# Interleaved state-space layers: residual and gate sums by accumulating DMA, another operand order in a short convolution, norm statistics by tile

## The chip, the cores and the metric

One core of a Trainium2 chip runs the whole program. Its engines work side by side, each through its own queue in order: TensorE (PE; weight loads are listed apart as PEld), VectorE (DVE), ScalarE (ACT), GpSimd (POOL) and SyncE (SP, which here only issues DMAs). The metric is the device time of one execution in microseconds. A profile is one execution recorded by the hardware; its span runs from the first to the last instruction.

## The reference

The input x has 2048 tokens of 640 channels. Four residual layers follow each other, A, B, A, B, with the same weights in both rounds:

```python
x = x + A(layernorm(x));  x = x + B(layernorm(x));  x = x + A(layernorm(x));  x = x + B(layernorm(x))

# A: diagonal complex recurrence over tokens, 640 states
Lam_bar = exp(exp(log_dt) * Lam);  B_bar = ((Lam_bar - 1) / Lam)[:, None] * Bmat
h_t = Lam_bar * h_(t-1) + B_bar @ u_t;  A(u)_t = 2 * real(Cmat @ h_t) + u_t * Dskip

# B: gate by a long convolution that does not depend on x
k_shift = causal convolution of k with shift_k (4 taps);  kv = k_shift * v
B(u) = u * (causal convolution of kv with ssm_k (2048 taps) + kv * ssm_D)
```

Since the gate of B does not depend on x, it is computed once ("the y part") and used by both B layers.

## The kernel before, in words

**Order.** Nothing is scheduled while the program is built. Every piece of work is a named task with an engine, and the string `ORDER` lists the tasks; `Sched.run` emits them in that order, so each engine's queue is the order's subsequence. A suffix `/a` or `/d` puts an evacuation or a normalise on ACT or DVE. `PLACE` gives every buffer its place in one SBUF arena, and every PSUM buffer its banks. Both were written out ahead by a planner; the numbers beside the tasks (estimates, `LAT`, `DMA`, and `SWD` in the change) were its costs and are not used when the program is built.

**The y part** works in five slices of 128 channels (`y_pass`, names `yq0` to `yq4`). First the short convolution and the product with v are made (`kv_tasks`, names `kv_`): k and v are loaded transposed, channels on partitions; per slice and half of the tokens eight products of 512 columns (L1025) with a diagonal matrix of one tap as stationary operand are summed in PSUM, and DVE multiplies by v (L1031). The result goes to a scratch tensor `kvd` in DRAM (`kv_st`, L1035) and comes back (`yqN_vl`, L1124) with 128 consecutive tokens of one channel to a row, a layout in which a Fourier transform can be done by matrix products: stage A with a small table `FA` (L1063, products that use 64 rows of the array), stage B with cosines and sines (L1087 to L1092). The same is done for ssm_k, the spectra are multiplied on DVE (L1138 to L1143), transformed back (L1162, L1163, an on-chip transpose, L1190), and stored to `ysd`. The table `FA` is made by POOL, DVE and ACT (`yt_f0` to `yt_f4`).

**The A layers** (`ALayer.chunk`, names `A1cN_` and `A2cN_`) work in four chunks of 512 tokens, and a chunk has four tiles q of 128 tokens on partitions and 640 channels. Statistics of a tile give the norm (`_ln`), `_id` applies it, a DMA transposes the chunk (`_tu`), `_bp` multiplies by the input weights (L635, L638), `_ev` evacuates, DVE rotates (`_ri`), scans (`_sc`, L674), carries the state to the next chunk (`_cy`) and rotates back (`_ro`), `_cp` multiplies by the output weights (L726), one PSUM group for a tile, and `_xe` evacuates the tile into the f32 residual x, with the sum over channels as a side result (`sums`). A layer 1 loads x a second time (`_xr`, L1293) and adds it as one more product with the identity matrix within L726; its `_xe` is then a plain copy, on ACT (L734) or DVE (L736). A layer 2 adds x during the evacuation, on DVE alone (L738). Layer 1 takes its statistics from one task for a chunk, on DVE (`bn_stats`, L569, L570); all others (`ln_stats`) take the mean from `sums` (L539) and run a square with an accumulator on ACT for each tile (L544).

**The B layers** (`b_chunk`, names `B1cN_` and `B2cN_`) normalise a tile (`_u`), multiply the chunk by the gate Y loaded from `ysd` (`_mm`, L783) and add (`_m`): B1 adds into x on DVE and takes the sums for the next norm (L789), B2 adds into Y on DVE (L791) and stores Y to the output (L754). The last chunk of B2 goes tile by tile with its own two DVE operations (L768, L772).

The products of all layers share the PSUM banks: a product starts when the evacuation of what its banks held has been done.

Of the kernel before, what the change touches and what calls it, by code (L numbers as in the profile page):

```python
# [9 lines left out]
ALU = mybir.AluOpType  # L10
# [7 lines left out]
P = 128  # L18
L = 2048
# [31 lines left out]
ARENA = 3216  # L51

ORDER = """
    warm yt_io0 kv_kd kv_lk0 kv_dsl yt_io6 a_pl yt_ph0 yt_io12 yt_ph6 a_ldB0 yt_h0 yt_sin0 yt_f0 yt_ph12 a_p0 a_ldB1 kv_k0 kv_d0 yt_sin6 yt_f2 kv_d1 kv_k1
    yq0_kl a_p1 a_b00:4 kv_d2 a_p2 kv_k2 kv_ds0 yt_sin12 yt_h1 kv_ds4 kv_lv0 a_b01:4 a_b00:0 a_b01:3 a_b0e1:4/a a_p3 kv_ds1 kv_mm0:0 a_wl00:0 a_b0e1:3/a
    yq0_ka yt_neg12 a_b0e0:0/a yt_neg0 a_b00:1 kv_lk1 a_p4 yt_f3 a_b01:1 a_b0e0:4/a yt_f4 a_b0e1:1/a a_b0e0:1/d kv_mm0:1 a_p5 yt_neg6 kv_ev0:0 a_wl00:1
    kv_ds2 yq0_KA:m2 kv_lv1 kv_ev0:1 yq0_KA:m3 yq0_KA:m0 yq0_KA:e2/a a_p6 a_ti a_b00:3 yq0_KA:e0/a a_dd yq0_KA:m1 a_lamd kv_st0 yq0_KA:e1/a kv_mm1:1
    a_b0e0:3/a kv_ds3 a_ta yt_Ci yq0_KA:e3/d kv_mm1:0 kv_ev1:1 a_b00:2 yq0_KB:m3 kv_ev1:0 a_b0e0:2/a yq0_vl a_t0 yq0_KB:e3/a a_b10:4 a_b01:2 a_b0e1:2/a
    yq0_KB:m1 a_b1e0:4/a yq0_KB:m2 a_f yq1_kl yq0_KB:e1/a a_b11:2 yq0_KB:e2/a yq0_KB:m0 a_b1e1:2/a yq0_KB:m4 a_b10:1 yq0_KB:e0/a kv_st1 yq0_VA:m1
    yq0_KB:e4/d a_b1e0:1/a yq0_VA:e1/d yq0_VA:m3 yq0_VA:m2 yq0_VA:e3/a yt_Si a_b11:4 yq0_VA:e2/d a_b11:1 a_b1e1:4/a yq0_VA:m0 a_b1e1:1/a a_b10:0  # L60
    yq0_VA:e0/d a_wc00:0 a_b10:3 a_b10:2 a_b1e0:0/a a_wm00:0 yq0_VB:m0 a_b1e0:3/a a_wl02:0 a_b1e0:2/d yq0_VB:m1 yq0_VB:e0/a yq1_ka kv_lk2 yq1_KA:m2
    yq0_VB:e1/a yq1_KA:m3 yq0_VB:m2 yq1_KA:e2/d yq1_KA:e3/a yq1_KA:m1 yt_nsi yq1_KA:m0 a_wl02:1 yq0_VB:e2/a yq0_VB:m3 yq1_KA:e1/d yq1_KA:e0/a kv_lk3
    yq0_VB:m4 yq0_VB:e3/d a_b01:0 yq0_VB:e4/a yq1_KB:m0 yq0_pw yq1_KB:m3 yq1_KB:e0/a a_wl01:1 yq1_KB:m2 yq1_KB:e3/a yq1_KB:m1 kv_lv2 yq1_KB:e2/a a_b11:0
    yq1_KB:e1/a kv_mm2:0 a_b0e1:0/a a_wl01:0 a_b1e1:0/a yq1_KB:m4 a_wc02:0 a_b11:3 kv_lv3 kv_mm2:1 a_b1e1:3/a yq1_KB:e4/a a_wc00:1 a_wm02:0 yq0_IB:m3
    yq1_vl a_wc01:0 kv_ev2:0 yq0_IB:m2 yq0_IB:e3/a kv_ev2:1 yq0_IB:m1 yq0_IB:e2/a yq2_kl yq0_IB:m0 a_wm01:0 yq0_IB:e1/a yq0_IB:m4 a_wm00:1 kv_mm3:0
    a_wc01:1 yq0_IB:e0/d yq0_IB:e4/a kv_st2 yq1_VA:m1 yq1_VA:m2 kv_ev3:0 yq1_VA:m0 yq1_VA:e1/a yq0_tt yq1_VA:e0/d yq1_VA:e2/a yq1_VA:m3 kv_mm3:1
    yq1_VA:e3/a a_wm01:1 yq2_ka yq1_VB:m4 yq2_KA:m2 kv_ev3:1 yq1_VB:m2 yq1_VB:e4/a yt_h2 yq2_KA:e2/a yq1_VB:m1 yq1_VB:e2/d a_wc02:1 yq1_VB:m0 yq1_VB:e1/a
    yq2_vl yt_h3 yq2_KA:m1 yq1_VB:m3 yq1_VB:e0/d yq2_KA:e1/a yq2_KA:m3 yq1_VB:e3/d yq2_KA:e3/a yq2_KA:m0 kv_lk4 yq0_IA:m1 yq1_pw yq2_KA:e0/a yq0_IA:m0
    yq0_IA:e1/a yq2_KB:m0 yq0_IA:e0/a yq2_KB:m4 yq2_KB:m2 kv_lv4 yq2_KB:e0/a yq2_KB:m1 yq2_KB:e2/a yq2_KB:m3 yq2_KB:e4/a yq2_KB:e1/a yq2_VA:m2 a_wl03:1
    kv_mm4:1 yq2_KB:e3/a a_wl03:0 yq2_VA:e2/a yq2_VA:m1 yq2_VA:m0 a_wl04:1 yq2_VA:e1/a kv_ev4:1 yq1_IB:m1 yq2_VA:e0/a a_wl04:0 yq1_IB:m4 yq1_IB:m2  # L70
    yq1_IB:e1/d yq1_IB:e4/a a_wc03:0 yq3_kl yq1_IB:m0 a_wm02:1 yq1_IB:e2/a yq2_VA:m3 yq1_IB:m3 a_wm03:0 yq1_IB:e0/a yq2_VA:e3/d kv_mm4:0 a_wc04:0 kv_st3
    a_wc03:1 a_wm04:0 yq1_IB:e3/a yq2_VB:m1 kv_ev4:0 a_wl10:1 a_wc04:1 yq2_VB:m0 yq2_VB:e1/a yq3_ka yq2_VB:m2 a_wm03:1 yq1_tt yq2_VB:e0/a a_wm04:1
    yq2_VB:m4 yq2_VB:m3 yq2_VB:e4/a yq2_VB:e2/a a_gm0 yq2_VB:e3/d yq2_pw yq3_KA:m0 yq3_KA:m2 a_wl10:0 a_ge0/a yq3_KA:m1 yq3_KA:e0/a a_gm1 xl0 yq3_KA:e1/a
    yq3_KA:e2/a a_wl11:0 yq1_IA:m1 a_ge1/a yq3_KA:m3 xl1 yq1_IA:m0 a_wc10:0 a_gm4 yq3_KA:e3/a A1c0_ln_bn yq1_IA:e0/a yq4_kl yq1_IA:e1/a yq3_KB:m1 a_ge4/a
    yq2_IB:m1 yq3_KB:e1/a kv_st4 yq2_IB:m3 yq2_IB:e1/a A1c1_ln_bn yq2_IB:m2 A1c0_ln_sd a_wl11:1 yq2_IB:m4 a_gm3 yq3_vl yq2_IB:e4/a yq2_IB:e3/a yq2_IB:e2/a
    A1c0_ln_post yq2_IB:m0 a_wc11:0 a_wm10:0 yq0_st yq3_KB:m4 a_ge3/a yq3_KB:m3 yq4_ka yq2_IB:e0/d a_wc10:1 a_gm2 A1c0_id:3/d A1c1_ln_sd A1c0_id:2/a
# [74 lines left out]
    "A1c3_pc1": 1, "A1c3_pc2": 4, "A1c3_pc3": 0, "A2c0_pb0": 2, "A2c0_pb1": 0, "A2c0_pb2": 7, "A2c0_pc0": 2, "A2c0_pc1": 6, "A2c0_pc2": 4, "A2c0_pc3": 6,  # L151
    "A2c1_pb0": 2, "A2c1_pb1": 6, "A2c1_pb2": 1, "A2c1_pc0": 3, "A2c1_pc1": 1, "A2c1_pc2": 5, "A2c1_pc3": 6, "A2c2_pb0": 0, "A2c2_pb1": 2, "A2c2_pb2": 4,
    "A2c2_pc0": 1, "A2c2_pc1": 5, "A2c2_pc2": 0, "A2c2_pc3": 3, "A2c3_pb0": 0, "A2c3_pb1": 3, "A2c3_pb2": 2, "A2c3_pc0": 5, "A2c3_pc1": 4, "A2c3_pc2": 2,
    "A2c3_pc3": 6,
}


# [1189 lines left out]
```

## Time and profile before

| | |
|---|---|
| median of 3 executions | 352.57 us (351.45 to 352.75) |
| profiled execution | 351.24 us, its span 349.0 us |
| PE busy | 325.5 us (93%) |
| DVE busy | 328.5 us (94%) |
| ACT busy | 241.5 us (69%) |
| POOL busy | 19.3 us (6%) |
| moved by DMA | 45.91 MB, 118712 packets |

In lines of groups, a row names source line, engine, operation, output and input with shapes, count, then busy us and the mean ns of one, then the idle time of the engine just ahead of them and what ended it. Busy time of a group is the time in which at least one of its instructions ran; matmuls overlap in the pipeline, so their mean duration (219 ns for 128 columns) is longer than the distance from one to the next. Stretches are given in microseconds from the start of the span. The chain of work is followed back from the last instruction to what released it.

### The profile page before, as it was taken

Reading aid. Unit: us, or ns where it says so; the run is one execution under the profiler, and the core shown is the slowest. Engines: PE = TensorE matmul, PEld = TensorE weight load, DVE = VectorE, ACT = ScalarE, POOL = GpSimd, SP = SyncE. Lnnn points to the kernel's source line nnn. Section 1 sums busy time; section 2 is a strip of 40 time slices with the busy share of each in tenths; the row PEclk is TensorE's granted clock in tenths of the full one; section 3 lists DMA queues with packets and bytes.
Section 4 is the critical chain, followed back from the end, with each engine's and each line's share of the span. In section 5 each row is a group of like instructions: output and inputs, shape, how many; then the busy total and the mean of one; then the engine's idle time right before and its main releaser. Section 6 shows DMA issues by size and latency. Waiting matters only on the chain.

```text
span 349.0 us, 8399 instructions
## 1 busy us (share of the span) xinstructions
PE 325.5 (93%) x3533; PEld 246.0 (70%) x3565; DVE 328.5 (94%) x504; ACT 241.5 (69%) x383; POOL 19.3 (6%) x51
## 2 busy tenths in 40 slices
PE   6669998999999999999999999999999999999990
PEld 6437976777686998896776685686868758755550
DVE  8989899898999999999989999999989989999996
ACT  5999998899899999563585598286317727307561
POOL 7590000000000000000000000000000000000000
PEclk9899999999999999999999999999999999999996
DMA  7999999999999977497067800306064040000204
GB/s 221 210 215 219 150 169 234 213 151 223 217 252 190 201 160 135 97 264 230 30 120 123 289 28 2 75 2 153 0 141 162 2 77 0 2 0 3 82 34 188
DMA packets 118712, 45.91 MB, mean 132 GB/s; under 512 B 111629, under 2 KB 112914, under 8 KB 118674
## 3 DMA queue, kind: packets, MB, share of 16 engines
q1 hardware_dynamic: 118528, 45.36, 60.2%
q8 instruction: 28, 0.46, 0.5%
q14 instruction: 10, 0.08, 0.1%
q10 hardware_dynamic: 146, 0.01, 0.0%
HBM read 17.38 MB, written 7.86 MB: 72 GB/s over the span
## 4 chain that ended last, share of the span: by engine, by line
PE 70%; DVE 19%; ACT 5%; DMA 2%; issue 2%; ACTq 1%; DVEq 0%; SPq 0%
PE banks L726 31%; PE banks L635 11%; PE banks L638 11%; PE banks L470 4%; DVE arena L247 4%; ACT arena L245 3%; PE banks L1162 2%; PE banks L1163 2%; PE banks L1025 2%; DMA arena<-in_A_Dskip_dram 1%; DMA arena<-kvd 1%; DVE arena L1141 1%; DVE arena L1140 1%; DVE arena L1139 1%; DVE arena L1138 1%
## 5 line engine op out<-in xcount | busy, mean ns | idle before, releaser
L245 ACT ACTIVATE arena<-banks 128x1024 bf16<-128x1024 f32 (+4 forms) x145 | 120.5, 903 | 37.1 <-PE banks L638 13.3
L726 PE MATMUL banks<-arena 128*128 128x128 bf16 (+1 forms) x859 | 116.5, 290 | 1.1
L726 PEld LDWEIGHTS <-arena 128*128 128x128 bf16 x880 | 67.8, 98 | 48.3
L638 PE MATMUL banks<-arena 128*128 128x256 bf16 x400 | 56.7, 273 | 0.0
L635 PE MATMUL banks<-arena 128*128 128x256 bf16 x400 | 56.7, 273 | 0.0
L674 DVE TENSOR_TENSOR_SCAN arena<-arena 128x1290 bf16<-128x1290 f32 x16 | 44.6, 2832 | 0.2
L638 PEld LDWEIGHTS <-arena 128*128 128x128 bf16 x400 | 39.1, 98 | 4.5
L635 PEld LDWEIGHTS <-arena 128*128 128x128 bf16 x400 | 38.5, 98 | 4.2
L544 ACT ACTIVATE junk<-arena,nmean 128x640 bf16<-128x640 f32 x48 | 39.6, 826 | 1.3
L1087 PE MATMUL banks<-arena 128*128 128x128 bf16 x170 | 35.1, 219 | 0.6 <-ACT arena L245 0.6
L1090 PE MATMUL banks<-arena 128*128 128x128 bf16 x170 | 35.4, 219 | 0.0
L247 DVE CAST arena<-banks 128x1024 bf16<-128x1024 f32 (+3 forms) x29 | 30.2, 1060 | 2.9 <-PE banks L1092 1.1
L1092 PE MATMUL banks<-arena 128*128 128x128 bf16 x150 | 32.8, 219 | 0.0
L1089 PE MATMUL banks<-arena 128*128 128x128 bf16 x150 | 32.8, 219 | 0.0
L589 ACT ACTIVATE arena<-arena,nmr,rstd 128x640 bf16<-128x640 f32 (+1 forms) x26 | 22.7, 912 | 7.4 <-DVE nmr L556 7.4
L539 ACT ACTIVATE nmean<-sums 128x4 f32<-128x4 f32 (+1 forms) x15 | 3.0, 203 | 31.7 <-DVE arena L738 28.2
L1025 PE MATMUL banks<-arena 128*128 128x512 bf16 x74 | 19.6, 397 | 3.4 <-ACT arena L245 2.9
L734 ACT ACTIVATE arena<-banks 128x640 f32<-128x640 f32 x12 | 8.4, 701 | 19.3 <-PE banks L726 19.3
L1162 PE MATMUL banks<-arena 128*128 128x128 bf16 x160 | 19.6, 219 | 0.5 <-ACT arena L245 0.5
L1163 PE MATMUL banks<-arena 128*128 128x128 bf16 x160 | 19.3, 219 | 0.6 <-DVE arena L1143 0.6
L591 DVE TENSOR_SCALAR arena<-arena,rstd,nmr 128x640 bf16<-128x640 f32 (+1 forms) x34 | 17.3, 543 | 0.1
L1087 PEld LDWEIGHTS <-arena 128*128 128x128 bf16 x170 | 16.6, 98 | 1.1
(201 smaller groups left out, 537.5 us busy)
## 6 DMA issues: line engine op xcount, KB each, us to landing
arena<-in_A_x_dram SPq DMA_DIRECT2D x8, 640.0 KB, 5.4
arena<-ysd SPq DMA_DIRECT2D x8, 640.0 KB, 4.9
arena<-in_B_ssm_k_dram SPq DMA_DIRECT2D x5, 512.0 KB, 6.4
kvd<-arena SPq DMA_DIRECT2D x5, 512.0 KB, 7.4
arena<-kvd SPq DMA_DIRECT2D x5, 512.0 KB, 5.1
ysd<-arena SPq DMA_DIRECT2D x5, 512.0 KB, 4.4
out_dram<-arena SPq DMA_DIRECT2D x8, 320.0 KB, 2.2
arena<-in_A_B_re_dram SPq DMA_DIRECT2D x1, 800.0 KB, 6.3
```

Of the source, the lines that this page charges most:

```text
L245: nc.scalar.activation(out, in_, ACT.Copy)
L247: nc.vector.tensor_copy(out, in_)
L544: nc.scalar.activation(small.junk, src(q), ACT.Square, bias=st["nmean"][:, i:i + 1], scale=1.0, accum_out=st["ssq"][:, i:i + 1])
L635: nc.tensor.matmul(pb[:, jj, c2, :], lhsT=bt1[:, c2, j, k, :], rhs=uT[:, 0:2, k, :], start=(k == 0), stop=False)
L638: nc.tensor.matmul(pb[:, jj, c2, :], lhsT=bt0[:, c2, k, j * P:(j + 1) * P], rhs=uT[:, 2:4, k, :], start=False, stop=(k == NJ - 1))
L674: nc.vector.tensor_tensor_scan(gv, rt, gv, 0.0, ALU.mult, ALU.add)
L726: nc.tensor.matmul(pc[:, o0:o1], lhsT=lh, rhs=rh, start=(n == 0), stop=(n == len(ops) - 1))
L1025: nc.tensor.matmul(pk[:, 512 * b:512 * (b + 1)], lhsT=s_ds.get()[:, l, :], rhs=kT[:, t0:t0 + 512], start=(l == 0), stop=(l == 3))
L1087: nc.tensor.matmul(ps[:, g, 0, :], lhsT=T["Cf"].get()[:, q, :], rhs=are, start=True, stop=single)
L1089: nc.tensor.matmul(ps[:, g, 0, :], lhsT=T["Sf"].get()[:, q, :], rhs=A[:, 2 * q + 1, :], start=False, stop=True)
L1090: nc.tensor.matmul(ps[:, g, 1, :], lhsT=T["NSf"].get()[:, q, :], rhs=are, start=True, stop=single)
L1092: nc.tensor.matmul(ps[:, g, 1, :], lhsT=T["Cf"].get()[:, q, :], rhs=A[:, 2 * q + 1, :], start=False, stop=True)
```

## The change

Five things change, and with them the whole of `ORDER` and `PLACE`, both written anew.

1. A layer 1 no longer reloads x and no longer adds it by an identity product. `_xe` copies PSUM into the f32 tile, and a new task `_xa`, a DMA issued from POOL's queue, adds the bf16 input from DRAM into that tile. A layer 2 does the same for chunks 0 to 2 with a separate f32 tile as source; chunk 3 keeps the sum on DVE.
2. The sums of B1, and those of B2 for chunks 0 to 2, become accumulating DMAs from POOL's queue (`_m`).
3. In the short convolution k becomes the stationary operand, in blocks of 64 channels by 128 tokens, and the diagonal matrix the moving one: the output has tokens on partitions, and 640 products of 64 columns take the place of 80 of 512. v is loaded plainly. The product is written so that a run of 4 channels lies together for each block of tokens, and an on-chip DMA transpose makes the layout for stage A; `kvd` is gone. Stage A of kv has a table of its own, `FV`, and both tables are made from 32 columns instead of 256.
4. Statistics are taken for each tile instead of for each chunk, on DVE (two `bn_stats` and one `bn_aggr`) or on ACT (two passes with an accumulator and three small operations), as the order says. A layer 2 now uses them too.
5. The mean for B1 and for B2's chunks 0 to 2 is the sum of what `_xe` summed and the mean that the A layer's statistics had, since the sum itself is now made by a DMA; it is made on DVE.

```diff
     DMA = ((1.3, 1.6), (0.8, 1.6))
     COLD = 5.0
+    SWD = (1.1, 3.0)
...
 def ln_stats(S, nc, small, src, sums, x_ready, name, qs, uses=(), base=None, parts=None):
...
+        if base is None:
+            nc.scalar.activation(st["nmean"][:], sums(), ACT.Copy, scale=-1.0 / D)
+        else:
+            nc.vector.scalar_tensor_tensor(st["nmean"][:], sums(), -1.0 / D, base(), ALU.mult, ALU.subtract)
...
 def bn_stats(S, nc, small, src, x_ready, name, uses):
+    for q in range(4):
+        def e_bn(eng, q=q):
+            mv, x = st["mv"], src(q)
+            if eng == "dve":
+                bs = small([P, 2, 6], "bs")
+                for h in range(2):
+                    nc.vector.bn_stats(bs[:, h, :], x[:, h * (D // 2):(h + 1) * (D // 2)])
+                nc.vector.bn_aggr(mv[:, q, :], bs[:])
+            else:
+                sm = small([P, 2, 6], "bs")[:, 0, :]
+                nc.scalar.activation(small.junk, x, ACT.Copy, accum_out=sm[:, 0:1])
+                nc.scalar.activation(sm[:, 1:2], sm[:, 0:1], ACT.Copy, scale=-1.0 / D)
+                nc.scalar.activation(mv[:, q, 0:1], sm[:, 0:1], ACT.Copy, scale=1.0 / D)
+                nc.scalar.activation(small.junk, x, ACT.Square, bias=sm[:, 1:2], accum_out=sm[:, 2:3])
+                nc.scalar.activation(mv[:, q, 1:2], sm[:, 2:3], ACT.Copy, scale=1.0 / D)
...
-                    if reload is not None:
-                        ops = ops + [(ident[:], resid(q)[:, d0:d1], d0, d1)]
...
+            if swd:
+                s_p = s_x[q] if dram is not None else S.slot(f"{nm}_p{q}", 4 * D, lambda t: t.bitcast(F32))
+
+                def e_xe(eng, q=q, s_pc=s_pc, s_p=s_p):
+                    if eng == "act":
+                        nc.scalar.activation(s_p.get(), s_pc.get()[:, 0:D], ACT.Identity, accum_out=sums_out()[:, q:q + 1])
+                    else:
+                        nc.vector.tensor_scalar(s_p.get(), s_pc.get()[:, 0:D], 1.0, 0.0, ALU.mult, ALU.add, accum_out=sums_out()[:, q:q + 1])
+                def e_xa(_, q=q, s_p=s_p):
+                    nc.gpsimd.dma_start(out=s_x[q].get(), in_=dram(q) if dram is not None else s_p.get(), accum_op=ALU.add)
...
                         if out is None:
-                            nc.vector.scalar_tensor_tensor(x, b, 1.0, x, ALU.mult, ALU.add, accum_out=sums_out()[:, q:q + 1])
+                            nc.gpsimd.dma_start(out=x, in_=b, accum_op=ALU.add)
                         else:
-                            nc.vector.tensor_tensor(s_Y.get()[:, q, :], b, x, ALU.add)
+                            nc.gpsimd.dma_start(out=b, in_=x, accum_op=ALU.add)
...
-            nc.sync.dma_start_transpose(out=s_vT.get(), in_=B_v[0][:, kb * P:(kb + 1) * P])
+            nc.sync.dma_start(out=s_v.get(), in_=B_v[0][:, kb * P:(kb + 1) * P].rearrange("(a i) d -> i a d", i=P))
...
-                for b in range(2):
+                for a in range(8):
                     for l in range(4):
-                        t0 = KPAD + 1024 * h + 512 * b - l
-                        nc.tensor.matmul(pk[:, 512 * b:512 * (b + 1)], lhsT=s_ds.get()[:, l, :], rhs=kT[:, t0:t0 + 512],
-                                         start=(l == 0), stop=(l == 3))
+                        t0 = KPAD + P * (8 * h + a) - l
+                        for r in range(2):
+                            rs = slice(64 * r, 64 * (r + 1))
+                            nc.tensor.matmul(pk[:, r, a], lhsT=kT[rs, t0:t0 + P], rhs=s_ds.get()[rs, l, rs],
+                                             start=(l == 0), stop=(l == 3))
...
         def e_vl(_):
-            nc.sync.dma_start(out=s_xv.get(), in_=rows(kvd[c0:c0 + DQ, :]))
+            nc.sync.dma_start_transpose(out=s_xv.get(), in_=s_kv.get())
```

## The prediction

> **What bounds the kernel now.** I read the page's first part, then busy time by stretch, then the waits of TensorE inside the long stretch, then the groups by line and form. The page:
>
> ```profile
> PE 325.5 (93%) x3533; PEld 246.0 (70%) x3565; DVE 328.5 (94%) x504; ACT 241.5 (69%) x383; POOL 19.3 (6%) x51
> ```
>
> Two engines are nearly full; which one sets the end differs by stage. I cut the span where the first A product (L726) starts, at 159.45 in the chain, and where the last matmul ends, 340.1. Columns: stretch, its length, busy us (instructions) of PE, PEld, DVE, ACT, POOL, clock, DMA share, GB/s.
>
> ```profile
> 0.00:119.70 119.70, 106.47 (x1535) 84.65 (x1547) 111.04 (x208) 107.99 (x142) 19.34 (x51) 0.99 1.05 204
> 119.70:159.45 39.75, 39.40 (x477) 35.80 (x475) 38.20 (x45) 32.98 (x42) 0.00 (x0) 1.00 0.78 168
> 159.45:340.10 180.65, 179.59 (x1526) 125.57 (x1545) 173.62 (x242) 99.13 (x196) 0.00 (x0) 1.00 0.29 73
> 340.10:349.00 8.90, 0.02 (x1) 0.00 (x0) 5.66 (x12) 1.42 (x4) 0.00 (x0) 0.69 0.47 184
> ```
>
> From 119.7 to 340.1 TensorE's list of waits has one line:
>
> ```profile
> PE banks L1162 <- ACT arena L245: 0.3, 1, 0.3
> ```
>
> It is also at its rate there: the chain has the 30 products of an even A tile in 4.08 us and the 25 of an odd one in 3.00. Pricing all work behind the first A product by such rows (32 tiles 113.3, their 16 identity products 4.35, input products 58.9, the last y slice 4.5) gives 181.1 against 180.65 measured. So the second part is a TensorE queue without holes: what leaves it shortens the span, what DVE is spared there doesn't. The first part is not TensorE's (131 us of its work in 159.45): DVE is busy 149.2 and ACT 141.0, and the DMA engines are full to 120. The tail of 8.9 is the last tile's normalise and store.
>
> Rows used below (DVE, then ACT, then PE):
>
> ```profile
> L789 DVE SCALAR_TENSOR_TENSOR arena<-arena 128x640 f32<-128x640 bf16 x16 | 12.4, 822 | 0.1
> L791 DVE TENSOR_TENSOR arena<-arena 128x640 bf16<-128x640 bf16 x12 | 9.5, 820 | 0.0
> L738 DVE SCALAR_TENSOR_TENSOR arena<-banks,arena 128x640 f32<-128x640 f32 x16 | 12.9, 818 | 1.4 <-PE banks L726 1.4
> L569 DVE BATCH_NORM_STATS2 bs<-arena 128x6 f32<-128x320 bf16 x32 | 13.5, 462 | 0.0
> L570 DVE BATCH_NORM_AGGREGATE mv<-bs 128x2 f32<-128x12 f32 x16 | 3.3, 209 | 0.6
> L544 ACT ACTIVATE junk<-arena,nmean 128x640 bf16<-128x640 f32 x48 | 39.6, 826 | 1.3
> L544 ACT ACTIVATION_READ_ACCUMULATOR junk<-arena,nmean 128x1 f32 x48 | 9.0, 187 | 0.0
> L1025 PE MATMUL banks<-arena 128*128 128x512 bf16 x74 | 19.6, 397 | 3.4 <-ACT arena L245 2.9 <-issue 0.2
> ```
>
> [...] No DMA of that queue is in this trace; the nearest row is the output store, 320 KB in 2.2 us. [...] 8 products of 64 rows (L1063) take 0.40 us and 24 take 0.84, 27.5 ns each, half of the 55 of a full-height one.
>
> **The change, part by part.**
>
> Identity residual gone, A layer 1: 16 tiles lose a product of 512 (216 ns) and one of 128 (56 ns): 16 x 0.272 = -4.35 us on the path. The order also does all of chunk 2's input products before the first A product (4.36 us earlier) and one y slice's last products after (0.93 later), so the queue behind that point is 180.65 - 4.35 - 4.36 + 0.93 = 172.9 us. The four moved blocks now sit in the front, which has 28 us without TensorE work; there they cost nothing unless the front turns TensorE-bound.
>
> Shift convolution: 80 products of 512 (1.89 us per 8: 17.3 in sum with all at rate) become 640 of 64 columns, k stationary. Bound below: half of the L1063 pace, 14 ns, 9 us. Above: the pace of 64-column products with new weights each (L1190, 16 more in 0.45, 28 ns), 18 us. I take 14. Hidden in the front either way; without that cover -8 to +1.
>
> kv: five stores and five loads of 512 KB (median 7.4 and 5.1 us to landing) and five transposes from DRAM become five plain loads and five on-chip transposes (5.9). The V chain gets 12.5 - 5.9 = 6.6 us shorter per slice, and full DMA engines lose 5 MB. DVE waited for that load 0.2 us: I price this 0, at most -4 (part of the 10.2 us that DVE idles before 159.45). On SP each transpose holds the queue about 2.5 us, as the V transposes it replaces did (median 2.7).
>
> Sums by DMA: DVE loses L789 (12.4) and L791 (9.5). Of 16 layer-2 evacuations (0.81) 12 turn plain, 8 of them on ACT: DVE -6.4, ACT +8 x 0.9 = 7.2. Statistics: DVE does 19 tiles where it did 16, at (13.5 + 3.3)/16 = 1.05: +3.2. ACT loses 16 squares at 1.01 (-16.2) and 11 means at 0.2 (-2.2), and gains 13 tiles of two passes and three small operations, 2 x 1.01 + 0.6 = 2.6: +34. Shifted evacuations and normalises: DVE +5.1, ACT -4.4; seven means on DVE at 0.16, +1.1. Sums: DVE -18.9 to about 310, ACT +18 to 260. Both stay below the span, and most of DVE's relief lies in the TensorE-bound part: worth nothing.
>
> Front: up to the first A product the new order puts on DVE 162.7 us of instructions where the old has 160.7 (summing the rows' means; the old sum measured 149.2 as busy, so x0.93): +1.8, of which 4.2 is chunk 1's rotation, which that product doesn't need. On ACT 163.3 for 154.7: +7.8, so it would be busy 149 of about 158. Call the front 158.5, between 152 (shorter DMA waits, filter table ready sooner through fewer columns) and 164 (ACT as its bound).
>
> New waits: POOL issues 56 accumulating DMAs, each 128 x 640 into f32 (327,680 B) or bf16. [...] I take 3.4 as an estimate; below, 2.2 by the store row; above, 7.4 by the store on full engines. For the issue I take the 1.1 us that the diff's planner sets, unmeasured here. Four run in line on POOL: 4.4 against 3.3 on DVE. Behind a late one stand: that tile's statistics, at the head of ACT's or DVE's queue, and behind these the PSUM evacuations that free banks for TensorE. Tightest place: the last B1 sum of chunk 0 to that chunk's layer-2 input products. Between them TensorE has 4.36 + 3.00 + 2.18 + 4.08 + 4.08 = 17.7 us. The chain needs 1.1 + 3.4 + 2.6 (statistics) + 0.6 + 1.8 (normalise) + 4.8 (transpose, median in this part) = 14.3. Slack 3.4: covered at my value, a stall from a landing of 6.8 us on. Chunks 1 to 3 have 22 us or more. I put 2.5 us of stalls in, 0 to 20.
>
> Tail: last chunk's tiles stay on DVE; 8.9, with chunk 2's output sums landing beside it, 9.2.
>
> Sum: 158.5 + 172.9 + 2.5 + 9.2 = 343.1 span, against 349.0. The profiled run is 2.24 above its span (351.24) and the median 1.33 above that run (352.57): 346.7, so about **346.5 us, -1.7%**.
>
> **Rivals.**
> First, the front gains too: the DMA relief and earlier table give 152 to 154 and no stalls: 153 + 172.9 + 0 + 9 + 3.6 = 338.5. For it: DMA share 1.05 to 120 us. Against: DVE's listed waits there are nearly all PE or ACT.
> Second, a wait takes the place of the one removed and the change ends slower: accumulating DMAs land at 8 to 10 us ([...] slow read-modify-write), and statistics block the evacuations queued behind them. It decides from 6.8 us landing; at 9 us each chunk's A2 entry and the three B2 and A1 steps before it wait 2 to 3 us more, 4 chunks x about 4 us = 16: 357 to 362.
> Third, ACT (+7.8 in the front, +10 behind) becomes the front's bound at 164 with 3 us more of stalls: 352. The engine was 88% busy in that stage.
> That the change doesn't do what it says: the DMAs add where DVE did; nothing else reads as unmoved.
>
> **How the numbers follow.** Forecast 0.47 (342 to 350), first rival 0.21, third 0.10, second 0.22. The measurement tells 0.5%, 1.8 us, from no change. Range 336 to 360 leaves out half of the slowest case and the best tenth. Faster: 0.47 + 0.21 less an edge of the forecast = 0.66; within: the third's core and that edge, 0.10; slower 0.24.
>
> **What would show it.** Right: PE without holes from the first A product on, some 173 us to the last matmul; L726's identity group gone; DVE near 310, ACT near 260; POOL's DMAs landing in 3 to 4 us and hardly named in the waits. Wrong: ACT or DVE statistics waiting for an accumulating DMA over 10 us in sum, PE waiting for ACT's evacuations after 160 us, or a first A product outside 152 to 164.

## The result, and the profile after

The changed kernel takes **364.57 us** (median of 4, 362.77 to 366.33) where the kernel before takes 352.66 us (351.45 to 353.14): ratio 1.034, 95% interval 1.028 to 1.040. The prediction was 346.5 us with a range of 336 to 360, so both the direction and the range were wrong. The profiled execution took 362.77 us with a span of 361.0.

From the page of the kernel after: the engines' first line, three of the rows of GpSimd's DMA issues (busy us, mean ns), the share of GpSimd's queue in the DMA engines' time, and the landing times of its DMAs (KB each, median us).

```profile
PE 324.8 (90%) x4093; PEld 251.6 (70%) x4093; DVE 305.9 (85%) x472; ACT 253.3 (70%) x440; POOL 63.9 (18%) x104
...
q0 software_dynamic: 8064, 16.39, 24.0%
...
L757 POOL DMA_DIRECT2D arena<-in_A_x_dram x16 | 16.6, 1237 | 135.5 <-DVE arena L691 96.9
...
L812 POOL DMA_DIRECT2D arena<-arena x16 | 15.4, 1371 | 38.9 <-DVE arena L806 38.9
...
L757 POOL DMA_DIRECT2D arena<-arena x12 | 11.5, 1061 | 39.2 <-ACT arena L751 26.2
...
arena<-arena POOLq DMA_DIRECT2D x28, 320.0 KB, 7.8
arena<-in_A_x_dram POOLq DMA_DIRECT2D x16, 320.0 KB, 6.4
```

VectorE lost 22.6 us of work, more than was forecast, and the kernel still became slower. What to see is the last two lines, 7.8 and 6.4 us where 3.4 was taken.

The stretches of the kernel after, cut as in the prediction, at the first A product (L742 now) and at the last matmul (columns as there):

```profile
0.00:166.37 166.37, 149.11 (x2586) 130.62 (x2587) 149.22 (x259) 146.94 (x202) 14.29 (x48) 0.96 0.93 164
166.37:349.74 183.37, 175.71 (x1510) 121.03 (x1507) 151.24 (x202) 104.94 (x234) 48.11 (x56) 0.99 0.71 149
349.74:361.00 11.26, 0.00 (x0) 0.00 (x0) 5.43 (x14) 1.42 (x4) 1.47 (x2) 0.60 0.92 226
```

| stretch | before | forecast | after |
|---|---|---|---|
| to the first A product | 159.45 | 158.5 | 166.37 |
| from there to the last matmul | 180.65 | 172.9 + 2.5 | 183.37 |
| tail | 8.90 | 9.2 | 11.26 |
| span | 349.0 | 343.1 | 361.0 |

Every stretch is longer than before. In the middle one TensorE is busy 175.71 of 183.37 us, so 7.7 us are holes, for 1.1 before. Its waits there, and below them ScalarE's that name a DMA (us in total, times, longest):

```profile
PE banks L656 <- DMA arena<-arena: 4.6, 3, 3.2
PE banks L656 <- ACT arena L751: 1.6, 1, 1.6
PE banks L742 <- DVE arena L761: 1.1, 1, 1.1
```

```profile
ACT junk L582 <- DMA arena<-arena: 11.6, 4, 5.6
...
ACT junk L552 <- DMA arena<-in_A_x_dram: 7.9, 4, 4.1
ACT junk L552 <- DMA arena<-arena: 5.4, 3, 2.8
```

L582 and L552 are the statistics of a tile that a sum has to reach first: 24.9 us at the head of ScalarE's queue. The prediction had set "over 10 us in sum" as the mark of being wrong.

The largest hole shows how it comes about. First the DMA view of 246 to 257 us (the queues' packets, MB and share of the 16 engines, then issues with landing), then the same time in steps of 2 us:

```profile
q0 software_dynamic: 600, 1.38, 61.9%
q1 hardware_dynamic: 2594, 0.66, 38.4%
...
arena<-arena POOLq DMA_DIRECT2D x4, 320.0 KB, 8.7
arena<-in_A_x_dram POOLq DMA_DIRECT2D x3, 320.0 KB, 12.3
```

```profile
252.00:254.00 2.00, 1.70 (x19) 1.17 (x18) 2.00 (x2) 0.00 (x0) 0.06 (x1) 1.00 1.22 189
254.00:256.00 2.00, 0.00 (x0) 0.00 (x0) 2.00 (x1) 0.00 (x0) 0.00 (x0) 1.00 1.15 268
256.00:258.00 2.00, 1.09 (x6) 0.76 (x6) 1.97 (x7) 1.93 (x6) 0.00 (x0) 0.60 1.10 238
258.00:260.00 2.00, 2.00 (x12) 1.41 (x11) 0.92 (x4) 1.94 (x7) 0.86 (x1) 0.55 1.08 317
```

From 245.8 on GpSimd issues four sums of B1 and three of A layer 1 behind each other, and SP at 246.15 the transpose of chunk 1 for its second A layer (L656 are the products behind it). All share the 16 DMA engines, which are full (61.9 + 38.4%). The transpose reaches TensorE at 256.9, and TensorE has had nothing for 3.2 us. Then the clock column falls to 0.60 and 0.55 (in finer steps it is 0.50 from 256.4 to 259.8 us): the hole is paid for once more, as five of the input products then take 1.02 us where the same take 0.55 from 259.9 on. The wait is thus not only for a sum; the sums also delay what travels beside them. The five transposes of an A chunk behind the first A product are the same work in both kernels. How long one holds SP's queue (ns, least, median and most), before, then after, then after with all sums left out (the first run of the next section):

```profile
L619 SPq DMA_TRANSPOSE arena<-arena x5: 3013/3073/3675, 182.4 to 281.3; - x5
```

```profile
L640 SPq DMA_TRANSPOSE arena<-arena x5: 3122/4645/5151, 183.7 to 296.1; - x5
```

```profile
L640 SPq DMA_TRANSPOSE arena<-arena x5: 3027/3062/3629, 184.8 to 287.4; - x5
```

A landing is recorded for two of the five only: 4.8 and 4.9 us before, 5.8 and 8.5 after, 4.9 and 5.5 without the sums.

The tail: SP's list of waits from 340 us on has the output stores (L777) behind the sums of the last chunks.

```profile
SPq L777 <- DMA arena<-arena: 29.2, 3, 24.9
```

### The profile page after: what moved, and what is told of

It reads as the page before. It is cut to its first block, busy times and chain, and to the rows that moved or that the text cites. A ratio compares the mean times of both kernels' runs of the same rounds, so it can differ in the third digit from the quotient of the medians.

```text
span 361.0 us, 9640 instructions
## 1 busy us (share of the span) xinstructions
PE 324.8 (90%) x4093; PEld 251.6 (70%) x4093; DVE 305.9 (85%) x472; ACT 253.3 (70%) x440; POOL 63.9 (18%) x104
## 5 line engine op out<-in xcount | busy, mean ns | idle before, releaser
L250 ACT ACTIVATE arena<-banks 128x1024 bf16<-128x1024 f32 (+4 forms) x141 | 120.4, 920 | 21.9 <-PE banks L659 13.1
L742 PE MATMUL banks<-arena 128*128 128x128 bf16 (+1 forms) x880 | 115.1, 292 | 1.5 <-DVE arena L761 1.1
L742 PEld LDWEIGHTS <-arena 128*128 128x128 bf16 x880 | 66.7, 98 | 49.1 <-issue 1.8
L656 PE MATMUL banks<-arena 128*128 128x256 bf16 x400 | 57.7, 276 | 6.5 <-DMA arena<-arena 4.6
L659 PE MATMUL banks<-arena 128*128 128x256 bf16 x400 | 57.3, 274 | 0.0
L656 PEld LDWEIGHTS <-arena 128*128 128x128 bf16 x400 | 38.8, 99 | 12.2 <-issue 5.4
L659 PEld LDWEIGHTS <-arena 128*128 128x128 bf16 x400 | 39.4, 98 | 4.8
L757 POOL DMA_DIRECT2D arena<-in_A_x_dram x16 | 16.6, 1237 | 135.5 <-DVE arena L691 96.9
L552 ACT ACTIVATE junk<-arena,nmean 128x640 bf16<-128x640 f32 x32 | 26.4, 825 | 19.6 <-DMA arena<-in_A_x_dram 7.9
L1119 PE MATMUL banks<-arena 128*128 128x128 bf16 x170 | 35.6, 222 | 2.0 <-DVE arena L252 1.1
L751 ACT ACTIVATE arena<-banks 128x640 f32<-128x640 f32 x20 | 14.0, 699 | 32.0 <-PE banks L742 26.7
L1122 PE MATMUL banks<-arena 128*128 128x128 bf16 x170 | 35.9, 221 | 0.0
L1124 PE MATMUL banks<-arena 128*128 128x128 bf16 x150 | 33.0, 220 | 0.0
L1121 PE MATMUL banks<-arena 128*128 128x128 bf16 x150 | 33.0, 220 | 0.0
L605 ACT ACTIVATE arena<-arena,nmr,rstd 128x640 bf16<-128x640 f32 (+1 forms) x25 | 21.8, 913 | 3.8 <-DVE nmr L564 3.8
L812 POOL DMA_DIRECT2D arena<-arena x16 | 15.4, 1371 | 38.9 <-DVE arena L806 38.9
L1197 PE MATMUL banks<-arena 128*128 128x128 bf16 x160 | 19.8, 222 | 0.7 <-DVE arena L880 0.4
L1196 PE MATMUL banks<-arena 128*128 128x128 bf16 x160 | 20.0, 222 | 0.0
L757 POOL DMA_DIRECT2D arena<-arena x12 | 11.5, 1061 | 39.2 <-ACT arena L751 26.2
L419 ACT ACTIVATE arena<-arena,s_F 128x640 f32<-128x640 bf16 x20 | 16.5, 840 | 2.6 <-DMA arena<-in_A_C_im_dram 1.5
```

The lines of the kernel that those rows point to most:

```text
L250: nc.scalar.activation(out, in_, ACT.Copy)
L552: nc.scalar.activation(small.junk, src(q), ACT.Square, bias=st["nmean"][:, i:i + 1], scale=1.0, accum_out=st["ssq"][:, i:i + 1])
L656: nc.tensor.matmul(pb[:, jj, c2, :], lhsT=bt1[:, c2, j, k, :], rhs=uT[:, 0:2, k, :], start=(k == 0), stop=False)
L659: nc.tensor.matmul(pb[:, jj, c2, :], lhsT=bt0[:, c2, k, j * P:(j + 1) * P], rhs=uT[:, 2:4, k, :], start=False, stop=(k == NJ - 1))
L742: nc.tensor.matmul(pc[:, o0:o1], lhsT=lh, rhs=rh, start=(n == 0), stop=(n == len(ops) - 1))
L757: nc.gpsimd.dma_start(out=s_x[q].get(), in_=dram(q) if dram is not None else s_p.get(), accum_op=ALU.add)
```

## Experiments: what the sums cost

**All 56 accumulating DMAs left out.** The task stays in the order and emits nothing.

```diff
-                    nc.gpsimd.dma_start(out=s_x[q].get(), in_=dram(q) if dram is not None else s_p.get(), accum_op=ALU.add)
+                    pass
...
-                        if out is None:
-                            nc.gpsimd.dma_start(out=x, in_=b, accum_op=ALU.add)
-                        else:
-                            nc.gpsimd.dma_start(out=b, in_=x, accum_op=ALU.add)
+                        pass
```

> The changed kernel with all 56 accumulating DMAs left out (neither the residuals of the A layers nor the sums of B are added, so this prices the DMAs with all waits on them). Theory (the landing of 6 to 8 us stands in the path behind the first A product): the stretch from the first A product to the last matmul falls from 183.4 us to 173 to 175, no TensorE wait for a DMA is left there, the tail falls from 11.3 to about 9; the front stays at 166.4. Together 352 to 355 us. Rival (the new order and the spread over engines make the holes, whatever the sums cost): 361 to 366.

349.95 us (347.92 to 352.53), 14.6 less than with them, and below the 352 to 355 that the theory had. Its stretches:

```profile
0.00:167.50 167.50, 148.37 (x2586) 129.50 (x2586) 148.82 (x259) 147.28 (x202) 14.15 (x48) 0.97 0.89 163
167.50:340.82 173.32, 173.32 (x1510) 120.33 (x1507) 152.25 (x204) 104.72 (x234) 0.00 (x0) 1.00 0.28 68
340.82:348.40 7.58, 0.00 (x0) 0.00 (x0) 4.48 (x10) 1.42 (x4) 0.00 (x0) 0.84 0.56 216
```

The middle is 173.32 us with TensorE busy in all of it: the queue behind the first A product was priced at 172.9. So in this stretch the new order and the spread over engines leave no hole of their own; the sums make the 10.1 us between 173.3 and 183.4 (7.7 as holes, and 2.4 because TensorE is busy 175.7 us, in part at a lower clock, with what takes 173.3 here), and 3.7 of the tail. The front is not touched, 167.5: it is a loss by itself. And even with the sums for nothing the kernel is only 0.7% under the kernel before (0.990 to 0.995).

**Each half left out.** The same edit on the B sums alone, and on the A sums alone.

> Only the 28 sums of the B layers left out (the gate products are not added; the second B layer stores its product alone); the 28 sums of the A layers stay accumulating DMAs. With all 56 out it took 349.95 us, with the B sums on VectorE 366.87. Theory 1 (both groups hold the path, and fewer DMAs at a time also land sooner; VectorE's 23 us more ate the gain when it took them over): 355 to 360 us. Theory 2 (the A sums, ahead of each B layer's statistics, hold the path alone): 361 to 365 us, with the same waits of ScalarE's squares for the loads from the input.

> Only the 28 sums of the A layers left out (no residual is added in three quarters of the second A layer and in all of the first); the B sums stay DMAs. Theory 1 (both groups hold the path): 354 to 360 us. Theory 2 (the A sums hold it alone): 350 to 353 us. A third possibility (the B sums, ahead of the A layers' statistics and of their 4.8 us transposes, hold it alone): 362 to 365 us.

Without the B sums 352.55 us (-12.0), without the A sums 354.95 (-9.6); the middle is 175.8 and 177.8 us. The two gains add to 21.6 where both together give 14.6. Both groups hold the path, and each is cheaper without the other (2.6 us for the A sums alone, 5.0 for the B sums): with the B sums gone the A sums land in 5.6 and 4.3 us. The result for no_b_sums lies outside of what either theory had (355 to 360 the nearer), on the side of a larger gain; that of no_a_sums is what theory 1 had.

**Plain copies.**

```diff
-                    nc.gpsimd.dma_start(out=s_x[q].get(), in_=dram(q) if dram is not None else s_p.get(), accum_op=ALU.add)
+                    nc.gpsimd.dma_start(out=s_x[q].get(), in_=dram(q) if dram is not None else s_p.get())
```

and the same for `_m`.

> The same 56 DMAs from the same queue, but as plain copies over the destination in place of sums (so the sums are not made). Theory (reading the destination and adding in the DMA engine makes the landing slow): landing 3 to 4.5 us in place of 6.4 and 7.8, and 353 to 358 us. Rival (the way through GpSimd's queue and the load of the DMA engines make it slow): landing 5.5 us or more, 361 to 366 us.

356.28 us (-8.3), as the theory had it, though the copies from DRAM land in 5.1 us. From its page, the queue's share and the landing, then the middle stretch and TensorE's longest wait:

```profile
q0 software_dynamic: 7296, 16.39, 16.8%
...
arena<-arena POOLq DMA_DIRECT2D x28, 320.0 KB, 3.5
arena<-in_A_x_dram POOLq DMA_DIRECT2D x16, 320.0 KB, 5.1
```

```profile
165.75:346.42 180.67, 175.53 (x1510) 121.19 (x1507) 152.34 (x204) 104.52 (x234) 29.89 (x56) 0.99 0.61 155
...
PE banks L656 <- DMA arena<-arena: 3.9, 1, 3.9
```

The same bytes take 16.8% of 354.1 us over 56 DMAs, 1.06 us of all 16 engines each; as sums they take 24.0% of 361.0, 1.55 us each (means over 44 DMAs of 320 KB and 12 of 160). Four issued in line then need at least 4 x 1.55 = 6.2 us, an estimate, which is most of the 7.8. The 3.4 that the prediction took is close to the 3.5 of a plain copy between two tiles. Of the 14.6 us, 8.3 are the price of adding (with the issue, 0.54 us for a copy and 1.06 to 1.43 for a sum), and 6.3 that of the copies and their waits.

Those 6.3 us matter for the forecast. Here most DMAs land in about the time it had priced, and yet the middle is 7.3 us longer than without DMAs, with a largest hole of 3.9 us at the same products, and the kernel is slower than before (ratio 1.008, 1.004 to 1.013). A right landing alone would not have made the change a gain.

**The B sums back on VectorE.**

```diff
-                            nc.gpsimd.dma_start(out=x, in_=b, accum_op=ALU.add)
+                            nc.vector.tensor_tensor(x, x, b, ALU.add)
...
-                            nc.gpsimd.dma_start(out=b, in_=x, accum_op=ALU.add)
+                            nc.vector.tensor_tensor(b, b, x, ALU.add)
```

> Only the 28 sums of the B layers go back to VectorE (0.82 us each, 23 us in all); the 28 of the A layers stay DMAs. Theory (landing, and the B1 sums ahead of the second A layer's statistics above all): ScalarE's and VectorE's statistics of B1's output no longer wait (11.6 us of waits in the trace), the TensorE wait of 3.2 us goes, 357 to 361 us. Rival (VectorE is needed for other work there and becomes the bound): 364 us or more, TensorE waiting for VectorE.

366.87 us, 2.3 more than as DMAs, and 14.3 more than with these sums left out. So 23 us of VectorE work, in an order written without it, cost 14 us, with VectorE busy 166.1 of the 185.4 us of the middle. The theory's 357 to 361 fell, the rival's 364 or more held. In this order VectorE's relief from the B sums (14.3 us) is worth a little more than their DMAs cost (12.0); an order written for sums on VectorE, like that of the kernel before, is another matter.

**The tile sums as additions on GpSimd.** As above with `nc.gpsimd.tensor_tensor`, for A layer 2 too; the 16 sums from DRAM stay DMAs.

> The 40 sums between two tiles in SBUF made by GpSimd's own addition, in the place in the order where its DMA was issued; the 16 sums from DRAM stay DMAs. Theory (latency of the DMA): one addition should take 1 to 2.5 us (no row shows it; VectorE takes 0.82) where issue and landing took 8.9, so most of the holes close: 354 to 358 us. Rival (GpSimd and VectorE get into each other's way [...], or GpSimd's queue becomes the late one): 362 us or more, with VectorE's rows longer.

384.53 us, 20 more: the rival. From its page GpSimd's additions, then from the groups behind the first A product a VectorE row with two tiles in SBUF as inputs and one with a single tile; below them the same rows of the kernel after.

```profile
L815 POOL TENSOR_TENSOR arena<-arena 128x640 f32<-128x640 f32 x16 | 32.5, 2050 | 32.0 <-DVE arena L809 32.0
...
L760 POOL TENSOR_TENSOR arena<-arena 128x640 f32<-128x640 f32 x12 | 29.1, 2448 | 24.3 <-ACT arena L751 17.0
```

```profile
L680 DVE TENSOR_TENSOR arena<-arena 128x2560 bf16<-128x2560 bf16 x6 | 12.7, 2108 | 0.0
...
L607 DVE TENSOR_SCALAR arena<-arena,rstd,nmr 128x640 bf16<-128x640 f32 x22 | 12.3, 605 | 0.1
```

```profile
L607 DVE TENSOR_SCALAR arena<-arena,rstd,nmr 128x640 bf16<-128x640 f32 x25 | 14.0, 606 | 0.2
...
L680 DVE TENSOR_TENSOR arena<-arena 128x2560 bf16<-128x2560 bf16 x6 | 8.9, 1486 | 1.7 <-DMA arena<-arena 1.7
```

An addition takes 2.0 to 2.4 us, and the two-input row goes from 1.49 to 2.11 us while the one-input row keeps its mean of 0.61. Means hide what happens here. The same two lines by single instructions, from 166 us to the end (ns, least, median and most):

```profile
L680 DVE TENSOR_TENSOR arena<-arena x6: 1484/2082/2830, 184.5 to 330.8; 128x2560 bf16<-128x2560 bf16 x6
...
L607 DVE TENSOR_SCALAR arena<-arena,rstd,nmr x28: 440/607/1694, 177.3 to 364.9; 128x640 bf16<-128x640 f32 x25, 128x640 bf16<-128x640 bf16 x3
```

The three L680 beside no addition take 1.48 to 1.49 us, the three beside one 2.68 to 2.83. Of L607 only four meet an addition: the two that began before it keep their 0.61, the two that began during one take 1.66 and 1.69. So beside a GpSimd addition the row with two inputs took 1.8 to 1.9 times as long, and the row with one took 2.7 to 2.8 times as long when it began during the addition; why, the trace does not show. How much of the 20 us this makes, and how much that an addition takes GpSimd 2.0 to 2.4 us where VectorE's sums took 0.82, this run does not separate.

**The identity products alone replaced in the kernel before.** Part 1 for A layer 1 alone, in the old order: 16 accumulating DMAs, and the mean for B1 from both sums.

```diff
-                    if reload is not None:
-                        ops = ops + [(ident[:], resid(q)[:, d0:d1], d0, d1)]
...
+            if reload is not None:
+                def e_xa(_, q=q):
+                    nc.gpsimd.dma_start(out=s_x[q].get(), in_=reload(q), accum_op=ALU.add)
```

> The kernel before with one part of the change alone: no identity products in the first A layer (4.35 us of TensorE), 16 accumulating DMAs from the input in their place, the mean of the first B layer from both sums; order, places and all else as before. Theory 1 (16 DMAs by themselves land in about 5 us and the squares behind them have the cover): 347 to 350 us. Theory 2 (in an order without room for a landing the squares wait at the head of ScalarE's queue and evacuations behind them): 353 to 360 us, TensorE waiting for ScalarE after 160 us.

367.75 us, ratio 1.043. The first A product comes at 159.4 as before; behind it TensorE's and ScalarE's waits:

```profile
PE banks L725 <- DVE arena L737: 6.0, 1, 6.0
PE banks L725 <- ACT arena L245: 4.8, 1, 4.8
PE banks L639 <- DMA arena<-arena: 2.6, 1, 2.6
```

```profile
ACT nmean L540 <- DVE arena L737: 23.9, 3, 13.5
ACT junk L547 <- DMA arena<-in_A_x_dram: 13.4, 3, 9.4
...
ACT junk L547 <- DVE nmean L542: 11.4, 3, 4.9
```

These DMAs land in 5.1 us with the engines 37% busy in that stretch, so it is not throughput here: the squares (L547) stand at the head of ScalarE's queue until the sum is there, up to 9.4 us. Before the hole of 4.8 us TensorE waits for an evacuation that stands behind squares on ScalarE; before the one of 6.0, for one on VectorE that stands behind a step of the statistics (L557), which waits 7.3 us for the squares. Taking 4.35 us from the TensorE queue cost 15 (367.75 for 353.00), outside of the 353 to 360 of theory 2. Not all of it is the sums': the mean on VectorE (L542) is part of this run too and ScalarE waits 11.4 us for it, and TensorE is busy 181.3 us in this stretch at a mean clock of 0.97, where 179.6 were enough before for more products at 1.00.

## Experiments: why the first A product comes late

**Less TensorE work early, and late.** Three of four taps left out of the short convolution (480 small products, most before 80 us); and the second summand of stage B left out in five places behind 80 us.

```diff
-                    for l in range(4):
+                    for l in range(1):
```

> Three of the four taps of the short convolution left out: 160 products of 64 columns instead of 640, with as many fewer weight loads. Theory (the front is TensorE's from 80 us on, so all its work and holes before the first A product count): 480 products at 20.6 ns, 9.9 us, and the hole of 1.8 us inside such a group go: first A product at 154 to 157 us, 352 to 355 us in all. Rival (VectorE and ScalarE set the front, as the prediction had it): first A product at 165 to 167, 363 to 366 us.

```diff
                     single = (q == 0 or q == 16)
                     are = A[:, (0 if q == 0 else 1) if single else 2 * q, :]
+                    single = single or name in ("yq2_VB", "yq3_KB", "yq3_VB", "yq4_KB", "yq4_VB")
```

> The changed kernel with the second summand of 150 of stage B's products left out (imaginary parts, in slices 2 to 4; the gate is wrong by them): 150 products of 128 columns at 55.6 ns, 8.3 us of TensorE, all issued after 80 us of the span. Theory (TensorE is full from 80 us on, so what is taken there comes off one for one, where the 9.9 us of one_tap, most of it before 80 us, brought the first A product only 3.3 us forward): first A product at 157 to 159.5. Rival (VectorE or ScalarE set the pace up to the first A product): 163 or later.

362.87 and 365.17 us, the second without its slowest execution, 370.57, which is the one that was profiled. The first A product came at 163.0 and 163.4, about 3 us earlier for 9.9 and 8.3 us less work; the six other runs that leave this front as it is have it between 165.3 and 167.5, so 3 us are clear of the scatter, but not by much. one_tap lies between its theory and its rival, late_cut on the side of its rival, and neither got its TensorE work back one for one. The stretches to 80 us and from there to the first A product, after and then before, say in part why: TensorE is full from 80 us on in both kernels, but VectorE is busy 94% and 96% there too, so work taken from one leaves the other.

```profile
0.00:80.00 80.00, 63.28 (x1336) 57.03 (x1336) 68.25 (x147) 71.42 (x96) 14.29 (x48) 0.91 1.08 185
80.00:166.37 86.37, 85.83 (x1252) 73.58 (x1251) 80.97 (x113) 75.52 (x107) 0.00 (x0) 1.00 0.79 144
```

```profile
0.00:80.00 80.00, 67.89 (x961) 53.98 (x967) 72.92 (x136) 71.67 (x97) 19.34 (x51) 0.98 1.01 198
80.00:159.45 79.45, 77.98 (x1051) 66.46 (x1055) 76.31 (x117) 69.31 (x87) 0.00 (x0) 1.00 0.95 193
```

By 80 us the changed kernel has been busy 4.6 us less on TensorE and 4.7 less on VectorE, part of it at half clock (in finer steps the clock is 0.50 for 13.7 of the 80 us, and for 3.4 before), and 7.9 us more of TensorE's work waits behind, of which the moved input products less the y slice's are 3.4. The clock is also a rival for what the two cuts did not bring: up to the first A product its mean is 0.94 in both, where the kernel after has 0.96. Little of the gain reached the end (362.87 and 365.17 against 364.57): with the sums in place the middle took 187.3 us in one_tap.

**The short convolution with full-height products.** 320 products of 128 rows by 128 columns, and VectorE's product in 20 pieces for 10.

```diff
-                        for r in range(2):
-                            rs = slice(64 * r, 64 * (r + 1))
-                            nc.tensor.matmul(pk[:, r, a], lhsT=kT[rs, t0:t0 + P], rhs=s_ds.get()[rs, l, rs],
+                        nc.tensor.matmul(pk[:, a >> 2, a & 3], lhsT=kT[:, t0:t0 + P], rhs=s_ds.get()[:, l, :],
                                              start=(l == 0), stop=(l == 3))
```

> The shift convolution with 128 rows and 128 columns to a product: 320 products and weight loads in place of 640, each about 55 ns in place of 20.6, so 17.7 us of TensorE for 13.2 (and VectorE multiplies in 20 pieces for 10). Theory ([...] the holes that no wait explains lie 1021 instructions apart): those holes, 2.0 us in the changed kernel and 3.1 to 5.6 in the other runs, fall under 0.5 us, and the first A product comes within 2 us of 166.4 in spite of 4.5 us more work. Rival (the transposed load of k is late there): the holes stay and the first A product comes at 169 to 172.

366.15 us, first A product at 169.5. Each side was right in one half. In the list of TensorE waits the holes that nothing explains are gone from these products (2.0 us in the kernel after), as the theory had it; the weight loads still show 3.8 us of them in 2 (6.9 in 5), but nearly all of that is one stop in which the first of these products waits 3.5 us for ScalarE (L250). The front is 3.2 us longer, which is in the rival's 169 to 172, though the 4.5 us of added TensorE work may be the reason instead of a late load of k. What made the holes is not shown.

**Part 3 alone in the kernel before.** For slices 0 to 2 of 5: the new products, v loaded plainly, kv relaid on chip, `FV` and the smaller tables. (No place was free for the longer-lived tiles of slices 3 and 4.)

```diff
+                if kb < 3:
+                    pk = pk.rearrange("p (r q a e) -> p r a q e", r=2, a=8, e=4)
+                    for a in range(8):
+                        for l in range(4):
+                            t0 = KPAD + P * (8 * h + a) - l
+                            for r in range(2):
+                                rs = slice(64 * r, 64 * (r + 1))
+                                nc.tensor.matmul(pk[:, r, a], lhsT=kT[rs, t0:t0 + P], rhs=s_ds.get()[rs, l, rs],
+                                                 start=(l == 0), stop=(l == 3))
+                    return
...
+            if qd < 3:
+                nc.sync.dma_start_transpose(out=s_xv.get(), in_=kv_store[1].get())
```

> The kernel before with part 3 of the change alone, for slices 0 to 2 of 5 (k stationary in 384 products of 64 columns, v loaded plainly, kv relaid by an on-chip transpose, the table FV; slices 3 and 4 by the old way through kvd, since their places do not fit), order and places else as before. Theory 1 (part 3 brings the holes of the front: [...] the clock falls behind a hole, and the relaying transpose holds SP's queue): first A product at 162 to 166 us in place of 159, 355 to 359 in all. Theory 2 (the new order costs the front its 6.9 us, with more TensorE work placed ahead of the first A product and less done by 80 us): first A product within 1.5 us of 159, 350 to 354.

351.06 us, ratio 0.995 (0.994 to 0.997); first A product at 158.75: theory 2. Part 3 does not cost the front anything, for these slices and in the old order at least. What is left for the 6.9 us is the new order with the statistics in it; which of its moves does it was not tried.

## Experiments: a version that beats both

Three runs ask whether the TensorE queue of the kernel before can be shortened another way: VectorE adds the reloaded input while it evacuates, and the identity products of that tile go. For 16 tiles (with 16 normalises moved to ScalarE), 8 tiles (with 5), and only the 4 whose evacuation was VectorE's already.

```diff
-                    if reload is not None:
+                    if reload is not None and f"{nm}_xe:{q}/a" in ORDER:
                         ops = ops + [(ident[:], resid(q)[:, d0:d1], d0, d1)]
...
-                elif reload is not None:
-                    nc.vector.tensor_scalar(s_x[q].get(), s_pc.get()[:, 0:D], 1.0, 0.0, ALU.mult, ALU.add, accum_out=sums_out()[:, q:q + 1])
                 else:
```

> The kernel before with the identity products gone another way: all 16 evacuations of the first A layer on VectorE, which adds the reloaded input while it evacuates (0.82 us; 12 of them were ScalarE's), and 16 normalises of the first B and second A layer moved from VectorE (0.61) to ScalarE (0.91), which is half idle there. TensorE -4.35, VectorE +9.8 - 9.7, ScalarE -10.8 + 14.6. Theory (TensorE sets the stretch and the two others have room): 347.5 to 350 us. Rival (VectorE is as full as TensorE, 19.4 of each 20 us, and its evacuations come later than ScalarE's did): 352 us or more.

> As before_dve16, but only for chunk 1 and the four tiles whose evacuation VectorE did already: TensorE -2.2 us (8 identities), VectorE +3.3 - 3.0 (5 normalises to ScalarE). Theory: 349.5 to 351.5 us. Rival: 352.5 or more.

> The kernel before without the identity products of the four tiles whose evacuation VectorE did already: it adds the reloaded input in the same pass (0.82 us either way). TensorE -1.09 us, no other engine more. Theory (TensorE's queue sets the stretch): 351.0 to 352.0, ratio about 0.997. Rival (these four evacuations and what they release set it): 352.5 to 354.

370.20, 354.03 and 351.99 us: ratios 1.048 (1.045 to 1.052), 1.003 (1.002 to 1.005) and 0.9975 (0.996 to 0.999). With 4 tiles no engine got more work and the 1.1 us came out nearly whole (0.9); with 8 and 16, where the rivals held, the balanced sums of busy time were no help. In the run with 16, TensorE's two longest waits and what ScalarE's means wait for:

```profile
PE banks L726 <- ACT arena L245: 5.6, 1, 5.6
PE banks L635 <- DVE arena L736: 4.2, 1, 4.2
```

```profile
ACT nmean L539 <- DVE arena L736: 50.9, 7, 13.5
```

In the kernel before VectorE is busy 173.6 of these 180.65 us and TensorE 179.6, so neither has much room. Ahead of the 4.2 us the evacuation (L736) stands behind two scans on VectorE; ahead of the 5.6 us ScalarE's evacuations stand behind squares and the normalises that were moved there. So both moves cost, whatever the totals are; the run does not separate them.

Part 3 for three slices and these 4 tiles together:

> Both gains together in the kernel before: part 3 for slices 0 to 2 (alone 351.06, ratio 0.995) and no identity product where VectorE evacuates anyway (alone 351.99, ratio 0.9975). If they act on different stretches they add: 349.8 to 350.6, ratio about 0.993. Rival (both only shift the same wait): 351 or more.

**349.54 us**, ratio 0.989 (0.987 to 0.991) to the kernel before, which took 353.31 us beside it: faster than both kernels. The two gains multiplied are 0.993, within what their intervals and this one allow. Its stretches, with the first A product at 159.3 and the middle 0.6 shorter than before:

```profile
0.00:159.32 159.32, 144.66 (x2346) 125.01 (x2355) 149.01 (x258) 140.58 (x183) 15.48 (x48) 0.98 1.02 185
159.32:339.33 180.01, 178.91 (x1521) 125.02 (x1539) 173.81 (x243) 99.15 (x197) 0.00 (x0) 1.00 0.28 73
```

Whether the two together bring more than their sum, and where in the span part 3 gains, these runs do not tell.

## The prediction, step by step

- **The accumulating DMA's landing, 3.4 us (bounds 2.2 to 7.4): this step failed.** Medians 7.8, 6.4 and, for B2's 160 KB, 6.3. The 3.4 was the author's estimate, between two store rows; no row showed a sum. It was priced as one transfer with nothing beside it. What counts is how long each holds the DMA engines, 1.55 us, and that four to seven are issued in line together with transposes and loads. The point named as deciding, 6.8 us, was passed by the first. By the plain copies this step is worth 8.3 us, more than the 6 us of gain that were forecast; but with the copies the kernel is slower too, so it did not decide the direction alone. The issue, taken as 1.1 us, was near: 1.06 to 1.43.
- **The stalls, 2.5 us (0 to 20): failed, though inside the bounds.** 10.1, by the run without sums, and 2.4 more in the tail than before, 3.7 more than without sums. The sign named for being wrong was there, statistics waiting 24.9 us on ScalarE. The place was wrong: chunk 0's chain, which was called tightest, costs a hole of 0.9 us, and the largest, 3.2, is at chunk 1's layer-2 input products, which were said to have 22 us of cover. The chain was priced with transposes at 4.8 us; the two that are recorded took 5.8 and 8.5, and without the sums 4.9 and 5.5. A consequence of the change on a transfer it doesn't touch was left out, and it would have stood with a right landing too: plain copies that land in 3.5 and 5.1 us still leave 7.3 us in this stretch.
- **The TensorE queue, 172.9 us:** right, 173.3 without the sums; so are its terms, the identity's 4.35 and the moved blocks.
- **The front, 158.5 us (152 to 164): failed**, at 166.4. The failing sentences are that the front "has 28 us without TensorE work" and that the moved blocks "cost nothing unless the front turns TensorE-bound". The prediction's own two lines had TensorE busy 145.9 of 159.45 us, so 13.6 were free and not 28, and the cut at 119.7 hid that 12.1 of them lie before 80 us. From there on TensorE was full already (78.0 of 79.45 us), with VectorE close behind, and by the queue's own sum what was taken out of the middle came back in front. That is a sum and no experiment: no run moved these blocks back, and cuts of 8 to 10 us of TensorE work brought only 3. Beyond these 3.4 us the slower start is put down to the order, by exclusion of part 3 only; the cause stays open.
- **The convolution, 14 us, hidden:** 13.2 by its row. kv priced at 0: in the kernel before, three slices of it gain 0.5% (1.8 us), inside the bound of -4.
- **VectorE -18.9, ScalarE +18:** -22.6 and +11.8. The sizes were near; that VectorE's relief is worth nothing was too strong for the new order, where 23 us put back cost 14.
- **The tail, 9.2:** 11.3; the last stores wait on SP for chunk 2's sums, and without sums it is 7.6.
- **The rivals:** the second named the mechanism (a landing beyond 6.8 us, statistics ahead of evacuations) and gave 357 to 362. The landing that it named, 8 to 10 us, was not reached, and its slow addition within the DMA fits the plain copies (1.06 us of the DMA engines each, 1.55 as sums). It had 0.22; it deserved more, as the forecast rested on a landing time that no row showed. The third named the front's loss (164), but with ScalarE as the cause, which no run singles out. The two came together, which no case held, so the time fell outside the range.

## What to carry to other kernels

Before a sum moves from an engine to a DMA, price how long it fills the DMA engines, times how many are issued in line, and look at which other transfers land in that time: here 1.55 us each, four to seven in line, and medians of 7.8 and 6.4 us where 3.4 was priced for one alone. Where the trace shows two engines full (TensorE 179.6 and VectorE 173.6 of 180.65 us here), busy time taken from a third or moved between them says little: with sums that balanced, before_dve16 took 370.20 us for 353.00. What stood at the head of an engine's queue and what waited behind it decided there. Cut a stretch where the holes of the engine end, not where a phase ends, before calling its free time cover.

## What was not expected of the hardware

- An accumulating DMA of 128 x 640 held the 16 DMA engines 1.55 us in the mean (1.50 with the B sums alone, 1.66 with the A sums alone), the plain copy of the same bytes 1.06; with sums in line, a transpose beside them held SP's queue 4.6 us, without them 3.1.
- The TensorE clock fell after a hole: 3.2 us without a product at 254 to 257 were followed by 0.60 and 0.55 in the next 4 us, and the 1.84 us of the next point by 0.50 and 0.69. In finer steps it is 0.50 from 256.4 to 259.8 us and from 61.8 to 65.2, about 3.4 us each time, and 1.00 on both sides. Behind the hole of 1.6 us at 207.6 it stayed at 1.00. The prediction priced holes at their length alone.
- In the middle of a group of 64-row products TensorE stopped for up to 1.84 us with no wait to name (3.5 in b_sums_dve); two such holes lie 1021 to 1026 instructions apart, by how a weight load ahead of its product is counted. These products took 20.6 ns each in the mean (13.2 us for 640), and each has a weight load of its own. In kv_full, with 320 full-height products, these holes are gone; no run shows what made them.
